# Two chunks share a slot of quarter products: the attention part of a fused retention and gated-FFN kernel, rearranged

## The chip, the cores and the metric

The kernel runs on one core of a Trainium2 chip. The metric is the device time of one execution in microseconds (us). A core has TensorE (PE in the profile; its weight loads are PEld), VectorE (DVE), ScalarE (ACT), GpSimd (POOL) and SyncE (SP), each with an instruction stream of its own that runs in order. Matrix products are accumulated in the eight banks of PSUM; the other operands lie in SBUF.

## What is computed

A retention layer (attention without softmax, with a decay in place of it) over 8 batches, 8 heads, 576 positions and 64 elements per head, and behind it a gated feed-forward network on its 4608 rows of 512 elements:

```python
def _attn_ref(q, k, v):                       # each [8, 8, 576, 64], float32
    scores = (1/sqrt(64)) * q @ k.transpose(0, 1, 3, 2)
    gamma = 1.0 - 2.0 ** (-5.0 - arange(8))   # one decay per head
    rel = pos[:, None] - pos[None, :]
    Dmat = where(rel >= 0, gamma[:, None, None] ** rel, 0.0)
    return (scores * Dmat) @ v

def _moe_ref(x, w_gate, w_val, w_out):        # x [4608, 512]; weights 512x1536, 512x1536, 1536x512
    gate = 1.0 / (1.0 + exp(-(x @ w_gate)))
    val = x @ w_val
    return (gate * val) @ w_out
```

Because the decay is a power of the distance, retention can be worked out in chunks: within a piece of 64 positions by masked scores (intra), and from all earlier positions through a state, the sum of k times v over them (inter). The powers of gamma are multiplied into q and k when they are cast to bf16.

## The kernel before

Everything on the way is bf16 with fp32 sums. `xT` holds the output of retention, transposed, as the input of the network. The network works in blocks of columns of `xT` (256, 384, 384 and then 512 columns): for each block 12 pairs of h products (gate and value, one pair per 128 of the 1536 hidden elements), then output products, 128 rows at a time, in three pieces of four. The retention of later columns is done in between: 30 chunks of 128 positions, each of two pieces (`j` = 0, 1) of 64. The products of a chunk use quarters of the array (64x64), so four of them, one per quarter, lie beside each other. Row half `y` of the array takes its operands from partitions 64y to 64y+63; column half `x` writes partitions 64x to 64x+63.

One **slot** carries, in TensorE's order, the values of the chunk before (intra, then inter), and the scores and state products of the next one:

```python
    ROWS = [(qk_psum, "qk"), (qk_psum, "qk")]      # two banks
    VALS = [(pv_psum, "pv"), (tr_psum, "tr")]      # two banks; ffn_psum has three, st_psum one

    def scores(s):                                  # 16 quarter products
        t = turned[s]
        row_ps[s] = [pool.tile([P, 2, M, 64], FP32, tag=tag, ...) for i, (pool, tag) in enumerate(ROWS)]
        # row_ps[s][y][half(j), 0, m] = k piece j times q piece j, head m of half y

    def products(s):                                # 16: what piece j adds to the state
        # row_ps[s][j][half(y), 1, m] = k piece j times v piece j

    def mask(s):                                    # VectorE, twice: causal mask, to bf16 (probs)
        ...

    def intra(s):                                   # 16
        val_ps[s] = [pool.tile([P, M + 2, 64], FP32, tag=tag, ...) for i, (pool, tag) in enumerate(VALS)]
        # val_ps[s][j][half(x), kc] += v piece j times probs piece j; row half j writes bank j

    def inter(s):                                   # up to 16
        for u in range(2):
            for j in range(NJ):
                if before(s, j) is None:            # the first piece of a batch has no state
                    continue
                for y in range(2):
                    for x in range(2):
                        m = 2 * u + x
                        nc.tensor.matmul(val_ps[s][y][half(x), 2 * y + u if j == y else M + u, :],
                                         lhsT=before(s, j)[half(y), m, :], rhs=turned[s][half(y), 0, m, half(j)],
                                         start=False, stop=(u == 1), skip_group_check=True)

    def slot(s):
        if s > 0:
            intra(s - 1)
            inter(s - 1)
        if s < NS:
            scores(s)
            if STEPS[s][1] < LAST:                  # the last chunk of a batch makes no state
                products(s)
        if s < NS:
            mask(s)
```

Row half `y` writes bank `y` only. Where `j` differs from `y`, the sum belongs to the other bank's values; it goes to two columns of its own (`M + u`), the **share**, and is added when the values are taken out. After a slot, its follow-up work is handed out in three steps, one after each of the next pieces of the network:

```python
    def leave_own(s, j):
        own = slice(2 * j, 2 * j + 2)
        nc.scalar.copy(out=xT[:, own, cols_of(s, j)], in_=val_ps[s][j][:, own])
        if before(s, j) is not None:
            shares[s, j] = nat_pool.tile([P, 2, 64], FP32, tag="share", ...)
            nc.scalar.copy(out=shares[s, j], in_=val_ps[s][1 - j][:, M:M + 2])

    def leave_other(s, j):                          # VectorE: the other two columns plus the share
        ...

    def add_state(s, j):                            # VectorE: running state + row_ps[s][j][:, 1], fp32
        ...

    def after(s, i):                                # i = 0, 1, 2
        makes = s < NS and STEPS[s][1] < LAST
        to_bf16 = on_act if s < 6 else on_pool
        if i > 0 and s > 0:
            leave_other(s - 1, i - 1)
        if i < 2 and s > 0:
            leave_own(s - 1, i)
        if i < 2 and makes:
            add_state(s, i)
        if i > 0 and makes and (s, i - 1) in totals:
            keep_state(..., totals.pop((s, i - 1)), to_bf16)     # the state in bf16
```

The main loop spreads the slots evenly over the pieces of a block:

```python
    BLOCKS = [(512, 256), (768, 384), (1152, 384)] + [(t, 512) for t in range(1536, NT, 512)]
    for w, (t0, n) in enumerate(BLOCKS):
        ...                                         # end: slots by which the next block's columns are ready
        for i, cols in enumerate(ffn_units(t0, n)):
            gone += cols
            ...
            if n > 256 and i % 2 and i < 2 * NFC:
                continue                            # only between a pair of h products and the next
            if pending:
                pending.pop(0)()
            elif slots < end and gone * (end - begin) >= (slots - begin) * (total - 5 * 2048):
                next_slot(slots)                    # slot(s), casts for chunk s + 3, three steps of after
                slots += 1
```

Casting a chunk takes GpSimd three instructions (k, q, v); q and k are then transposed by a DMA into the tile T.

Of the kernel before, what the change touches and what calls it, by code (L numbers as in the profile page):

```python
# [16 lines left out]
def kernel(  # L17
# [268 lines left out]
    def cast_v(s, eng):  # L286
        natural["v", s] = nat_pool.tile([P, H, D], BF16, tag="v", name=f"v_{s}")
        eng(out=natural["v", s], in_=loaded[s][2])  # L288

    def cross(s):  # L290
        t = att_pool.tile([P, 2, M, P], BF16, tag="T", name=f"T_{s}", bufs=5)
        nc.sync.dma_start_transpose(out=t.rearrange("p j m t -> p (j m) t"),
                                    in_=natural_qk[s].rearrange("p j m d -> p (j m d)"))
        turned[s] = t
# [27 lines left out]
    def pair_qk(A, g, banks):  # L322
# [8 lines left out]
        if g == 0:  # L331
            probs["p", A] = att_pool.tile([P, 2, M, 2, P], BF16, tag="ptp", name=f"ptp_{A}", bufs=2)
        for hh in range(2):
            nc.vector.tensor_tensor(out=probs["p", A][:, hh, 2 * g:2 * g + 2], in0=ps[hh],  # L334
                                    in1=trip.unsqueeze(1).to_broadcast([P, 2, 2, P]), op=ALU.mult)
# [33 lines left out]
    def third_intra(banks):  # L369
# [4 lines left out]
        for r in range(2):  # L374
            for u in range(2):
                for y in range(2):
                    for a in range(2):
                        for x in range(2):
                            kc = 2 * y + u
                            nc.tensor.matmul(pair_ps[4 + a][kc][0][half(x), kc, :],  # L380
                                             lhsT=natural["v", 2][half(a), r, head(2, 2 * u + x, y), :],
                                             rhs=probs["p", 2][half(a), y, 2 * u + x, r, :],
                                             start=(a, x) not in begun, stop=(r == 1 and kc == M - 1),
                                             skip_group_check=True)
                            begun.add((a, x))
# [21 lines left out]
    def pair_intra(A, g, a):  # L407
# [3 lines left out]
        for i in range(2):  # L411
            m = 2 * g + i
            ps, at_m, of = pair_ps[s][m]
            for r in range(2):
                for hh in range(2):
                    nc.tensor.matmul(ps[half(hh), at_m, :], lhsT=natural["v", A][half(a), r, 2 * m + hh, :],
                                     rhs=probs["p", A][half(a), hh, m, r, :],
                                     start=(at_m == 0 and r == 0), stop=(at_m == of - 1 and r == 1),
                                     skip_group_check=True)
# [18 lines left out]
    def turn_step(s):  # L438

        t = att_pool.tile([P, 2, M, P], BF16, tag="T", name=f"T_{s}", bufs=5)  # L440
        for i, ((pool, tag), eng) in enumerate(zip(VALS, (on_act, on_dve))):
# [10 lines left out]
    def new_state(key, dt=BF16):  # L452
        final = dt == BF16 and key[1] == LAST - 1 and key[2] == NJ - 1
        tag = "s32" if dt == FP32 else "sf" if final else "sb"
        return nat_pool.tile([P, M, D], dt, tag=tag, name=f"{tag}_{key[0]}_{key[1]}_{key[2]}", bufs=4)

# [18 lines left out]

    def scores(s):
        t = turned[s]
        row_ps[s] = [pool.tile([P, 2, M, 64], FP32, tag=tag, name=f"row_{s}_{i}") for i, (pool, tag) in enumerate(ROWS)]
        for m in range(M):
# [14 lines left out]
    def mask(s):  # L494
        probs[s] = att_pool.tile([P, 2, M, 64], BF16, tag="pt", name=f"pt_{s}")
        for y in range(2):
            nc.vector.tensor_tensor(out=probs[s][:, y], in0=row_ps[s][y][:, 0],  # L497
                                    in1=tri.unsqueeze(1).to_broadcast([P, M, 64]), op=ALU.mult)

    def intra(s):  # L500
        val_ps[s] = [pool.tile([P, M + 2, 64], FP32, tag=tag, name=f"val_{s}_{i}") for i, (pool, tag) in enumerate(VALS)]
        for kc in range(M):
            for j in range(NJ):
                for x in range(2):
                    h = 2 * kc + x
                    nc.tensor.matmul(val_ps[s][j][half(x), kc, :], lhsT=natural["v", s][half(j), h, :],  # L506
                                     rhs=probs[s][half(j), h // M, h % M, :], start=(kc == 0), stop=(kc == M - 1),
                                     skip_group_check=True)

    def inter(s):  # L510


        for u in range(2):
            for j in range(NJ):
                if before(s, j) is None:
                    continue
                for y in range(2):
                    for x in range(2):
                        m = 2 * u + x
                        nc.tensor.matmul(val_ps[s][y][half(x), 2 * y + u if j == y else M + u, :],  # L520
                                         lhsT=before(s, j)[half(y), m, :], rhs=turned[s][half(y), 0, m, half(j)],
                                         start=False, stop=(u == 1), skip_group_check=True)

    def slot(s):

        if s > 0:
            intra(s - 1)
            inter(s - 1)
        if s < NS:
            scores(s)  # L530
            if STEPS[s][1] < LAST:
                products(s)
        if s < NS:
            mask(s)

    def leave_own(s, j):

        own, other = slice(2 * j, 2 * j + 2), slice(2 - 2 * j, 4 - 2 * j)
        nc.scalar.copy(out=xT[:, own, cols_of(s, j)], in_=val_ps[s][j][:, own])  # L539
        if before(s, j) is not None:  # L540
            shares[s, j] = nat_pool.tile([P, 2, 64], FP32, tag="share", name=f"share_{s}_{j}", bufs=4)
# [26 lines left out]
    def after(s, i):  # L568

        makes = s < NS and STEPS[s][1] < LAST  # L570
        to_bf16 = on_act if s < 6 else on_pool
        if i > 0 and s > 0:
            leave_other(s - 1, i - 1)
        if i < 2 and s > 0:
            leave_own(s - 1, i)
        if i < 2 and makes:
            add_state(s, i)
        if i > 0 and makes and (s, i - 1) in totals:
            b, c = STEPS[s]
            keep_state((b, c, i - 1), totals.pop((s, i - 1)), to_bf16)  # L580

# [30 lines left out]
    def next_slot(s):  # L612
# [6 lines left out]
        if s + 1 == 1:  # L619
            pending.insert(2, lambda: turn_step(s + 1))  # L620


# [316 lines left out]

    BLOCKS = [(512, 256), (768, 384), (1152, 384)] + [(t, 512) for t in range(1536, NT, 512)]  # L940
    pieces = 0
    slots = 0
    for w, (t0, n) in enumerate(BLOCKS):
        nxt = BLOCKS[w + 1] if w + 1 < len(BLOCKS) else None
        end = last_step(nxt[0] + nxt[1]) + 2 if nxt else NS + 1
        begin = slots
        total = 2 * NFC * 4 * n + 12 * 512 * (n // P)
        gone = 0
        for i, cols in enumerate(ffn_units(t0, n)):
            gone += cols  # L950
            pieces += 1
            if stores and (nxt is None or w + 2 == len(BLOCKS) and pieces % 4 == 0):
                leave()
            if n > 256 and i % 2 and i < 2 * NFC:
                continue
            if pending:
                pending.pop(0)()
            elif slots < end and gone * (end - begin) >= (slots - begin) * (total - 5 * 2048):
                next_slot(slots)
                slots += 1  # L960
        while pending or slots < end:
            if pending:
                pending.pop(0)()
            else:
                next_slot(slots)
                slots += 1
    while stores:
# [30 lines left out]
```

## Time and profile before

| | |
|---|---|
| time, three runs | 332.96, 334.00, 334.78 us; median 334.0 |
| span of the profiled execution | 330.1 us, TensorE clock 1.00 throughout |
| TensorE busy | 320.9 us |
| h products (two groups) | 100.0 and 100.6 us of busy time |
| output products (512 columns each) | 81.2 us, 379 ns for one |
| quarter products: intra | 480 of 198 ns (overlapping), 9.9 us of busy time |
| mask (VectorE) | 60 of 419 ns |
| gv, the gated product (VectorE) | 96 of 654 ns on average |
| sigmoid (ScalarE) | 96 of 570 ns on average |

A duration in the profile is that of one instruction. Matrix products overlap: the next one starts long before the record of the last ends, so what a product costs TensorE is read from the distance between starts, not from its duration. The timeline merges neighbouring instructions of one kind (x16 are sixteen), and gives the start of the first and the time to the end of the last. In a group, the number after the bar is busy time, the next the mean of one, and then the idle time ahead of it, with what ended it.

### The profile page before, as it was taken

Reading aid. Unit: us, or ns where it says so; the run is one execution under the profiler, and the core shown is the slowest. Engines: PE = TensorE matmul, PEld = TensorE weight load, DVE = VectorE, ACT = ScalarE, POOL = GpSimd, SP = SyncE. Lnnn points to the kernel's source line nnn. Section 1 sums busy time; section 2 is a strip of 40 time slices with the busy share of each in tenths; the row PEclk is TensorE's granted clock in tenths of the full one; section 3 lists DMA queues with packets and bytes.
Section 4 is the critical chain, followed back from the end, with each engine's and each line's share of the span. In section 5 each row is a group of like instructions: output and inputs, shape, how many; then the busy total and the mean of one; then the engine's idle time right before and its main releaser. Section 6 shows DMA issues by size and latency. Waiting matters only on the chain.

```text
span 330.1 us, 8965 instructions
## 1 busy us (share of the span) xinstructions
PE 320.9 (97%) x3663; PEld 172.1 (52%) x3696; DVE 154.9 (47%) x357; ACT 130.2 (39%) x322; POOL 117.2 (35%) x171
## 2 busy tenths in 40 slices
PE   8899999899999999999999999999999999999996
PEld 8764557756646654444444444444444444444443
DVE  6845647666616633552356326541555056304310
ACT  6554545454424433432343333432443233423321
POOL 5684545533545573244224606070434000000000
PEclk9999999999999999999999999999999999999999
DMA  7999999999999999999967897959414900020003
GB/s 215 313 371 370 332 266 218 181 181 160 192 197 164 208 185 267 195 181 260 164 129 101 214 199 92 167 152 191 74 34 110 333 7 2 0 97 33 1 34 95
DMA packets 144794, 55.16 MB, mean 167 GB/s; under 512 B 125168, under 2 KB 136688, under 8 KB 144752
## 3 DMA queue, kind: packets, MB, share of 16 engines
q1 hardware_dynamic: 144608, 54.44, 79.7%
q8 instruction: 29, 0.48, 0.6%
q10 hardware_dynamic: 144, 0.13, 0.1%
q14 instruction: 13, 0.11, 0.1%
HBM read 37.75 MB, written 9.44 MB: 143 GB/s over the span
## 4 chain that ended last, share of the span: by engine, by line
PE 95%; ACT 2%; DVE 1%; issue 1%; ACTq 0%
PE h L638 50%; PE op L705 23%; PE op L892 3%; PE hv L742 3%; PE hg L742 3%; PE val L506 2%; PE idle L182 2%; PE row L490 1%; PE row L482 1%; PE val L520 1%; PE op L694 1%; PE qkp L329 1%; ACT qT L320 1%; PE hg L821 1%; PE st L348 1%
## 5 line engine op out<-in xcount | busy, mean ns | idle before, releaser
L638 PE MATMUL h<-xT,wv_sb 128*128 128x512 bf16 (+2 forms) x416 | 100.0, 355 | 0.8
L638 PE MATMUL h<-xT,wg_sb 128*128 128x512 bf16 (+2 forms) x431 | 100.6, 355 | 0.2
L666 DVE TENSOR_TENSOR gv<-g,h 128x512 bf16<-128x512 bf16 (+1 forms) x96 | 62.8, 654 | 65.1 <-PE h L638 62.4
L662 ACT ACTIVATE g<-h 128x512 bf16<-128x512 f32 (+1 forms) x96 | 54.8, 570 | 97.1 <-PE h L638 96.7
L705 PE MATMUL op<-wo_sb,gv 128*128 128x512 bf16 x361 | 81.2, 379 | 1.3 <-issue 1.1
L638 PEld LDWEIGHTS <-wg_sb 128*128 128x128 bf16 x432 | 41.9, 98 | 41.5 <-DVE xT L550 0.6
L638 PEld LDWEIGHTS <-wv_sb 128*128 128x128 bf16 x432 | 40.6, 98 | 37.3
L705 PEld LDWEIGHTS <-gv 128*128 128x128 bf16 x372 | 35.8, 98 | 42.1
L497 DVE TENSOR_TENSOR pt<-row,tri 128x256 bf16<-128x256 f32 x60 | 22.6, 419 | 63.1 <-PE row L490 55.7
L459 POOL CAST sb<-s 128x256 bf16<-128x256 f32 x35 | 14.0, 400 | 102.4 <-DVE s L563 70.4
L681 ACT COPY ob<-op 128x512 f32<-128x512 f32 x33 | 19.3, 585 | 56.7 <-PE op L705 51.2
L283 POOL TENSOR_TENSOR qk<-k,ktab 128x512 bf16<-128x512 f32 x30 | 31.3, 1042 | 23.1 <-DMA k<-in_k_dram 14.8
L283 POOL TENSOR_TENSOR qk<-q,qtab 128x512 bf16<-128x512 f32 x28 | 29.2, 1042 | 2.4 <-DMA q<-in_q_dram 1.8
L288 POOL CAST v<-v 128x512 bf16<-128x512 f32 x29 | 17.7, 609 | 10.7 <-DMA v<-in_v_dram 8.5
L550 DVE TENSOR_TENSOR xT<-val,share 128x128 bf16<-128x128 f32 x54 | 15.4, 285 | 9.0 <-ACT share L542 9.0
L539 ACT CAST xT<-val 128x128 bf16<-128x128 f32 x60 | 15.7, 263 | 8.7 <-PE val L520 8.7
L542 ACT COPY share<-val 128x128 f32<-128x128 f32 x54 | 15.3, 283 | 2.6 <-DVE xT L550 1.5
L563 DVE TENSOR_TENSOR s<-s,row 128x256 f32<-128x256 f32 x39 | 16.1, 412 | 0.0
L506 PEld LDWEIGHTS <-v 64*64 64x64 bf16 x480 | 6.4, 107 | 12.6 <-issue 12.3
L892 PE MATMUL op<-wo_sb,gv 128*128 128x512 bf16 x45 | 11.4, 379 | 0.3 <-issue 0.2
L506 PE MATMUL val<-pt,v 64*64 64x64 bf16 x480 | 9.9, 198 | 0.8 <-DVE xT L550 0.8
L334 DVE TENSOR_TENSOR ptp<-qkp,trip 128x512 bf16<-128x512 f32 x12 | 7.6, 684 | 4.6 <-PE qkp L329 4.6
(100 smaller groups left out, 240.2 us busy)
## 6 DMA issues: line engine op xcount, KB each, us to landing
out_dram<-ob SPq DMA_DIRECT2D x31, 256.0 KB, 3.1
k<-in_k_dram SPq DMA_DIRECT2D x26, 256.0 KB, 4.8
q<-in_q_dram SPq DMA_DIRECT2D x26, 256.0 KB, 4.6
v<-in_v_dram SPq DMA_DIRECT2D x26, 256.0 KB, 5.2
wg<-in_moe_w_gate_dram SPq DMA_DIRECT2D x12, 256.0 KB, 5.9
wv<-in_moe_w_val_dram SPq DMA_DIRECT2D x12, 256.0 KB, 5.5
wo<-in_moe_w_out_dram SPq DMA_DIRECT2D x12, 256.0 KB, 5.4
k32p<-in_k_dram SPq DMA_DIRECT2D x6, 256.0 KB, 5.5
```

The source lines that it names most:

```text
L283: eng.tensor_tensor(out=natural_qk[s][:, i].rearrange("p m (y d) -> p y m d", y=2), in0=by_halves(loaded[s][1 - i]), in1=tab, op=ALU.mult)
L288: eng(out=natural["v", s], in_=loaded[s][2])
L497: nc.vector.tensor_tensor(out=probs[s][:, y], in0=row_ps[s][y][:, 0], in1=tri.unsqueeze(1).to_broadcast([P, M, 64]), op=ALU.mult)
L506: nc.tensor.matmul(val_ps[s][j][half(x), kc, :], lhsT=natural["v", s][half(j), h, :], rhs=probs[s][half(j), h // M, h % M, :], start=(kc = ...
L563: nc.vector.tensor_tensor(out=new, in0=running[b], in1=p, op=ALU.add)
L638: nc.tensor.matmul(out, lhsT=w_sb[:, kc, fc * P:(fc + 1) * P], rhs=xT[:, kc, t0 + a:t0 + e], start=(kc == 0), stop=(kc == NKC - 1))
L662: nc.scalar.activation(out=g[:, 0:n], in_=h1[:, 0:n], func=AF.Sigmoid)
L666: nc.vector.tensor_tensor(out=gvs[some[0]][:, a:e], in0=g[:, 0:n], in1=h2[:, 0:n], op=ALU.mult)
L681: (eng or on_act)(out=ob, in_=opp)
L705: nc.tensor.matmul(opp, lhsT=gvs[fc][:, nb * P:(nb + 1) * P], rhs=wo_sb[:, fc, :], start=(fc == 0), stop=(fc == NFC - 1))
L742: nc.tensor.matmul(ps, lhsT=(wg_sb if what == "g" else wv_sb)[:, kc, fc * P:(fc + 1) * P], rhs=xT[:, kc, 0:4 * P], start=(kc == 0), stop=( ...
L892: nc.tensor.matmul(opps[nb], lhsT=gvs[fc][:, nb * P:(nb + 1) * P], rhs=wo_sb[:, fc, :], start=(fc == 0), stop=(fc == NFC - 1))
```

## The change

From the block at column 1152 on, a slot takes two chunks (`slot_of_two`), and it is placed among the output products only. The first three blocks keep 4, 3 and 1 single slots.

In a slot of two, the values of both chunks lie in the same two banks, eight columns of 64 in each, and there are no shares: each inter product adds straight to where its sum belongs. For that, both row halves write each bank[...]. So the inter products fall into two families: first those of a row half's own bank, behind the intra products; then VectorE reads one column of each bank (`glance`); then, after the scores and state products of the two new chunks, those of the other bank. The reads tie the two families: the second may only start when VectorE has seen the first. The values leave by one ScalarE copy per chunk and piece. The second new chunk's scores take the bank of `st` and one of the three `ffn` banks.

The single slots keep the shares, but ScalarE copies both in the first step of the follow-up work and its own columns later, so that ScalarE and VectorE read different banks at a time. Buffers grow: v from 5 to 6, T from 5 to 6 (shared with ptp, now two tiles in place of one), pt from 3 to 4, bf16 states from 4 to 8. The core of the diff:

```diff
@@ cast_v, cross, turn_step, new_state, mask: numbers of buffers, as above (cut)
-    def scores(s):
+    def scores(s, banks=None):
         t = turned[s]
-        row_ps[s] = [... for i, (pool, tag) in enumerate(ROWS)]
+        row_ps[s] = [... for i, (pool, tag) in enumerate(banks or ROWS)]
...
-    def inter(s):
+    def inter(s, js, apart=False):
         for u in range(2):
-            for j in range(NJ):
-                if before(s, j) is None:
-                    continue
-                for y in range(2):
+            for y in range(2):
+                for j in js[y]:
+                    if before(s, j) is None:
+                        continue
                     for x in range(2):
                         m = 2 * u + x
-                        nc.tensor.matmul(val_ps[s][y][half(x), 2 * y + u if j == y else M + u, :],
-                                         lhsT=before(s, j)[half(y), m, :], rhs=turned[s][half(y), 0, m, half(j)],
-                                         start=False, stop=(u == 1), skip_group_check=True)
+                        out_ = val_ps[s][y][:, M + u] if apart and j != y else val_ps[s][j][:, 2 * y + u]
+                        nc.tensor.matmul(out_[half(x)], lhsT=before(s, j)[half(y), m, :],
+                                         rhs=turned[s][half(y), 0, m, half(j)], start=False, stop=(u == 1),
+                                         skip_group_check=True)
...
+    ROWS_2 = [(st_psum, "st"), (ffn_psum, "ffn")]
+    glance = consts.tile([P, NJ], FP32)
+
+    def slot_of_two(vals, news):
+        if vals:
+            both = values(len(vals) * M, vals[0])
+            for i, s in enumerate(vals):
+                val_ps[s] = [t[:, i * M:(i + 1) * M] for t in both]
+                intra(s, i == 0)
+                inter(s, [(0,), (1,)])
+            for j in range(NJ):
+                nc.vector.tensor_copy(out=glance[:, j:j + 1], in_=both[j][:, 0, 0:1])
+        for s, banks in zip(news, (ROWS, ROWS_2)):
+            scores(s, banks)
             if STEPS[s][1] < LAST:
                 products(s)
+        for s in vals:
+            inter(s, [(1,), (0,)])
+        for s in news:
             mask(s)
 
+    def after_two(vals, news, i):
+        if i < NJ:
+            for s in vals:
+                nc.scalar.copy(out=xT[:, :, cols_of(s, i)], in_=val_ps[s][i])
+        for n, s in enumerate(news):
+            b, c = STEPS[s]
+            if c == LAST:
+                continue
+            if i == n:
+                add_state(s, 0)
+                add_state(s, 1)
+            if i == n + 1:
+                for j in range(NJ):
+                    if (s, j) in totals:
+                        keep_state((b, c, j), totals.pop((s, j)), on_act)
...
     def after(s, i):                     # single slots
-        if i > 0 and s > 0:
-            leave_other(s - 1, i - 1)
-        if i < 2 and s > 0:
-            leave_own(s - 1, i)
-        if i < 2 and makes:
-            add_state(s, i)
-        ...
+        if i == 0:
+            if s > 0:
+                leave_share(s - 1, 0)
+                leave_share(s - 1, 1)
+            if makes:
+                add_state(s, 0)
+        else:
+            if s > 0:
+                leave_other(s - 1, i - 1)
+                leave_own(s - 1, 2 - i)
+            if i == 1 and makes:
+                add_state(s, 1)
+            ...                          # keep_state as before
...
+    def next_two(vals, news):
+        slot_of_two(vals, news)
+        if news:
+            casts_to(news[-1] + LEAD_CAST + 1)
+        for i in range(3):
+            pending.append(lambda i=i: after_two(vals, news, i))
...
+    SINGLE = [4, 3, 1]
     for w, (t0, n) in enumerate(BLOCKS):
...                                      # twos: the pairs (vals, news) of this block, none for w < 2
             if pending:
                 pending.pop(0)()
             elif slots < end and gone * (end - begin) >= (slots - begin) * (total - 5 * 2048):
                 next_slot(slots)
+                valued = slots - 1
                 slots += 1
+            elif twos and i - n_h >= (0 if len(twos) > 1 else 5 if n < 512 else 6):
+                next_two(*twos[0])
+                valued = twos[0][0][-1]
+                slots = max([slots] + [s + 1 for s in twos.pop(0)[1]])
```

## The prediction

> **What bounds the kernel now.** I read the page from the top, first the busy shares and slices, then the chain that ended last and the groups:
>
> ```profile
> PE 320.9 (97%) x3663; PEld 172.1 (52%) x3696; DVE 154.9 (47%) x357; ACT 130.2 (39%) x322; POOL 117.2 (35%) x171
> ...
> PE   8899999899999999999999999999999999999996
> ...
> PEclk9999999999999999999999999999999999999999
> ...
> PE 95%; ACT 2%; DVE 1%; issue 1%; ACTq 0%
> ...
> L550 DVE TENSOR_TENSOR xT<-val,share 128x128 bf16<-128x128 f32 x54 | 15.4, 285 | 9.0 <-ACT share L542 9.0
> L539 ACT CAST xT<-val 128x128 bf16<-128x128 f32 x60 | 15.7, 263 | 8.7 <-PE val L520 8.7
> L542 ACT COPY share<-val 128x128 f32<-128x128 f32 x54 | 15.3, 283 | 2.6 <-DVE xT L550 1.5
> L563 DVE TENSOR_TENSOR s<-s,row 128x256 f32<-128x256 f32 x39 | 16.1, 412 | 0.0
> ```
>
> TensorE is busy in every slice, at full clock, and 95% of the chain is TensorE: the end is set by how long its in-order stream takes. VectorE and ScalarE are under half busy, so what the change saves there counts only where TensorE waits for it.
>
> Busy TensorE is not TensorE at its best, so I went to the TensorE timeline around two slots in a block of 512 columns:
>
> ```profile
> 125.19 1.03 PE L638 MATMUL h<-xT,wg_sb 128*128 128x512 bf16 x4
> 126.14 0.32 PE L506 MATMUL val<-pt,v 64*64 64x64 bf16 x16
> 126.29 0.30 PE L520 MATMUL val<-T,sb 64*64 64x64 bf16 x16
> 126.42 0.30 PE L482 MATMUL row<-T 64*64 64x64 bf16 x16
> 126.66 1.04 PE L638 MATMUL h<-xT,wv_sb 128*128 128x512 bf16 x3
> ...
> 132.71 1.03 PE L638 MATMUL h<-xT,wg_sb 128*128 128x512 bf16 x4
> 133.66 0.32 PE L506 MATMUL val<-pt,v 64*64 64x64 bf16 x16
> 133.81 0.30 PE L520 MATMUL val<-T,sf 64*64 64x64 bf16 x16
> 133.94 0.30 PE L482 MATMUL row<-T 64*64 64x64 bf16 x16
> 134.07 0.36 PE L490 MATMUL row<-v,qk 64*64 64x64 bf16 x16
> ```
>
> Four products of 512 columns start every 0.216 us: their merged 1.03 us is three steps and one duration of 0.379, and (1.03 - 0.379)/3 is 0.217. The group of 132.71 therefore starts its last at 133.36 and would let a next one start at 133.57. The slot's first quarter product starts at 133.66, **0.09 us late**. The 64 quarter products start over 0.58 us (133.66 to about 134.24, which is 134.07 + 0.36 less one duration of 0.19): 9 ns each. The next full-array product starts at 134.36, **0.12 us after the last quarter product**. A slot of 64 thus costs 0.79 us, of which about 0.20 is entering and leaving, if the last quarter's own 8 ns is left out. The slot at 126.14 lacks the products of L490: next due at 126.06, resumed at 126.66, 0.60 us for 48. Sixteen state products then cost 0.18 and the other kinds 0.13 each, which again leaves 0.20 for the two borders. (After most slots the trace lacks the record of one large product: 416 of 432 for wv, where all 432 weight loads are there. In the timeline that looks like 0.22 us lost; I don't count it.)
>
> Adding, over all pairs of neighbouring large products, what exceeds their normal step gives next to nothing beyond slots and missing records. One slot does wait, slot 2 in the 256-column block. The timeline of all engines there:
>
> ```profile
> 62.47 0.28 DVE L550 TENSOR_TENSOR xT<-val,share 128x128 bf16<-128x128 f32 x1
> ...
> 62.79 0.27 ACT L542 COPY share<-val 128x128 f32<-128x128 f32 x1 [0.53 <-DVE xT L550]
> 62.95 0.41 ACT L459 CAST sb<-s 128x256 bf16<-128x256 f32 x1
> 63.26 0.66 ACT L652 ACTIVATE g<-h 128x256 bf16<-128x256 f32 x2
> ...
> 63.67 0.42 DVE L654 TENSOR_TENSOR gv<-g,h 128x256 bf16<-128x256 bf16 x1 [0.59 <-ACT g L652]
> ...
> 64.01 0.28 DVE L550 TENSOR_TENSOR xT<-val,share 128x128 bf16<-128x128 f32 x1
> ...
> 64.35 0.31 PE L506 MATMUL val<-pt,v 64*64 64x64 bf16 x14 [0.84 <-DVE xT L550]
> ```
>
> ScalarE's copy of the second share waited 0.53 us for a VectorE reader of the same bank; cast, sigmoid, gv and the last xT add moved back with it, and TensorE lost 0.84 us before it could reuse the value bank.
>
> [...] 0.09 and 0.12 us at the borders, and no gap where L506, L520, L482 and L490 follow each other. [...] From the groups above, 412 ns at 256 columns and 285 at 128 leave 158 ns at zero columns; I use that.
>
> **The change, part by part.**
>
> *Fewer slots (on the path).* Before there are 31 slots (30 chunks, and the values trail by one). After: 4 + 3 + 1 single slots in the first three blocks, then two slots of two in each of the blocks from column 1152 to 3584, six blocks, so 12. 20 instead of 31: 11 pairs of borders fewer, 11 x 0.20 = **2.2 us less**. The number of quarter products is the same (16 + 16 + 16 + 16 a chunk, less where there is no state), at the same 9 ns.
>
> *The look (on the path only where it isn't covered).* In a slot of two, TensorE writes the intra products and the inter products of its own row half, then VectorE copies one column of each of the two banks, and TensorE's remaining inter products wait for that. From the last start of the first family: to VectorE's start 0.26 us (the slot at 149 shows 149.85 for the mask after a last product at 149.59); two looks of 0.158 us, the second starting about 0.08 after the first, as neighbouring masks start 0.34 apart at 0.42 each: 0.24; back to TensorE 0.06 (64.29 to 64.35 above). Round trip 0.56 us. Beneath it TensorE issues scores and state products of the two new chunks, 2 x (0.13 + 0.18) = 0.62: covered, with 0.06 to spare. I still charge 0.04 for each of eight such slots, since VectorE may be a little late. In three slots the second chunk is the last of a batch, whose L490 products are left out: 0.44 of cover, 0.12 lost each. The last slot of two has no new chunks: 0.56 lost. Sum 0.32 + 0.36 + 0.56 = **1.2 us more**.
>
> *Single slots reordered.* Both shares are copied ahead of the readers they waited for, and at later steps ScalarE and VectorE read different banks. In the stretch shown, the sigmoid could start some 0.6 us earlier, and so the release of the bank: **0.6 us less** of the 0.84. The other seven single slots show no wait worth more than 0.15, so there is nothing more to gain.
>
> *Off the path.* ScalarE's four reads of 263 and 283 ns per chunk become two of 128x256 (about 0.37 each); two VectorE adds of 285 go; the bf16 state casts move from GpSimd to ScalarE (0.41 each). In the output-product stretch these engines do little: from 148.05 to 159.40 VectorE is busy 2.6 and ScalarE 2.5 of 11.35 us. VectorE's train after a slot of two is 4 masks and 4 state adds at 0.34 apart, done some 4 us after the slot began; the next slot of two comes five or six output pieces of 0.86 later, 5.7 us at the least. Row banks, probabilities and states are then ready. The ffn bank lent to a row tile is free again by the same time, before its turn in the rotation of three.
>
> Sum: 334.0 - 2.2 + 1.2 - 0.6 = **332.4 us**.
>
> **Rivals.** *The look waits behind other work.* The first slot of two in a block comes one output piece (0.86 us) after the last h product; the last gv (0.69 us on VectorE, starting 0.27 after its product) is then just over, so VectorE is free when the look is due. If it were not, every first slot would lose up to 0.7 us: 6 x 0.7 = 4 us, and the time would be about 336. For it: the page puts VectorE waits at the door of ScalarE's sigmoid. Against it: the order just worked out.
>
> *Buffers or transfers tie the pairs together.* Two chunks ahead of use, six T and six v buffers are all full after each slot of two, and casts and transposes come in bursts. If a T came late, TensorE would stop for microseconds, and the time would be 335 to 340. Against it: a T is made at least one slot of two ahead, the first pair apart; GpSimd needs 2 x (1.04 + 1.04 + 0.61) = 5.4 us and a transpose 4.7 us of some 17 us a pair. For it: the DMA slices stand at 9 in the first half of the span.
>
> *Slots cost less among output products than among h products*, or first-half savings on VectorE and ScalarE open more waits than I see: 331. I found no such wait to open.
>
> **Range and chances.** The certain term is 2.2 us, 0.7% of the time; the terms against it are each under 1.5. Runs of the kernel before differ by 1.8 us among themselves, so the range is 330.8 to 334.2. 2% would be 6.7 us, three times all that borders can give: faster by over 2% 0.01, within 2% 0.96, slower by over 2% 0.03, which is the late T.
>
> **What would show it.** Right: 20 slots; among them 12 of two chunks (128 quarter products in a full one), each costing 0.20 for borders; TensorE idle before the second family of inter products near zero where two full chunks are new, about 0.1 in three slots, about 0.55 in the last; the wait of 0.84 at slot 2 down to 0.2 or 0.3. Wrong: idle before the second family of over 0.2 in most slots, a VectorE queue that holds gv or masks in front of the look, TensorE waiting for a T, or quarter products that take more than 9 ns in the new order.

## The result, and the profile after

The changed kernel takes 329.28 us (median; 329.05 to 329.44), the kernel before 333.56 beside it: a ratio of 0.9867, with a 95% interval of 0.9835 to 0.9898. That is 4.3 us less, within the 2% that the prediction called "within", and below its range of 330.8 to 334.2. The predicted gain was 1.6 us, so the prediction missed more than half of it. Measured once more on another occasion, the pair gave 329.17 against 332.41, ratio 0.9894 (0.9864 to 0.9925), 3.2 us; the changed kernel had stayed where it was. So about 1 us of the first 4.3 lay in the four executions of the kernel before, and some 3.2 us are to be explained.

The page of the kernel after, its busy shares, its slices, its chain by engine and the group of the look (count, then busy time, then the mean in ns):

```profile
PE 317.6 (97%) x3662; PEld 172.3 (53%) x3696; DVE 149.1 (46%) x335; ACT 139.3 (43%) x314; POOL 104.1 (32%) x138
...
PE   8899999999999999999999999999999999999995
...
PE 94%; DMA 1%; issue 1%; ACT 1%; DVE 1%; POOL 0%; SPq 0%; ACTq 0%
...
L553 DVE COPY glance<-val 128x1 f32<-128x1 f32 x24 | 2.7, 154 | 23.3 <-PE val L525 22.6
```

TensorE is still what sets the end, its busy time is 3.3 us shorter, and 24 looks of 154 ns have come in: two for each of 12 slots of two.

One such slot in the timeline of all engines (start, time to the end of the last, what):

```profile
145.60 0.32 PE L509 MATMUL val<-pt,v 64*64 64x64 bf16 x16
...
145.94 0.24 PE L525 MATMUL val<-T,sf 64*64 64x64 bf16 x8
...
146.00 0.34 PE L483 MATMUL row<-T 64*64 64x64 bf16 x16
...
146.25 0.22 DVE L553 COPY glance<-val 128x1 f32<-128x1 f32 x2 [0.65 <-PE val L525]
...
146.47 0.35 PE L491 MATMUL row<-v,qk 64*64 64x64 bf16 x16
...
146.64 0.27 PE L525 MATMUL val<-T,sb 64*64 64x64 bf16 x8
...
147.13 0.38 PE L765 MATMUL op<-wo_sb,gv 128*128 128x512 bf16 x1 [0.16 <-issue]
```

The first family ends with starts just before 146.00; VectorE looks from 146.25 to 146.47; the second family starts at 146.64, right behind the last state product (146.47 + 0.35, less one duration of 0.19, is 146.63). The look is covered. After the output product ahead of the slot, the next one was due at 145.51; it starts at 147.13, and 0.22 of that is an output product whose record is missing (355 of 372 are there). That leaves 1.40 us for 128 quarter products, where two single slots of 64 take 1.58: 0.18 less. A second trace of the changed kernel, in which that record is there, gives 1.40 as well.

The last slot of two has nothing new to do, and there the look is bare:

```profile
287.73 0.24 PE L525 MATMUL val<-T,sf 64*64 64x64 bf16 x8
...
288.02 0.23 DVE L553 COPY glance<-val 128x1 f32<-128x1 f32 x2 [3.92 <-PE val L525]
288.30 0.26 PE L525 MATMUL val<-T,sb 64*64 64x64 bf16 x8 [0.33 <-DVE glance L553]
```

The first family's last start is at 287.78 (0.24 less one duration of 0.19, behind 287.73), so the round trip is 0.52 us. The bracket counts only the 0.33 in which no product was in flight.

And slot 2, which had waited 0.84 us for its value bank:

```profile
62.29 0.26 ACT L583 CAST xT<-val 128x128 bf16<-128x128 f32 x1
62.42 0.42 DVE L714 TENSOR_TENSOR gv<-g,h 128x256 bf16<-128x256 bf16 x1
...
62.76 0.28 DVE L597 TENSOR_TENSOR xT<-val,share 128x128 bf16<-128x128 f32 x1
...
63.10 0.31 PE L509 MATMUL val<-pt,v 64*64 64x64 bf16 x14 [0.17 <-DVE xT L597]
```

ScalarE no longer waits here for VectorE's reader (0.53 us before). Counted from the slot's first quarter product (63.30 before, 62.72 here), the last xT add starts after 0.04 us where it had started after 0.71, and TensorE goes on after 0.38 in place of 1.05. In four other traces with the new order and the pairs this slot costs TensorE 1.13 us where it had cost 1.82. In the trace shown it costs 1.46, because 0.34 us pass between two of its state products, at 63.58; nothing in the trace says why.

### The profile page after: what moved, and what is told of

Same layout as the page of the kernel before. It is cut to its first block, busy times and chain, and to the rows that moved or that the text cites. A ratio compares the mean times of both kernels' runs of the same rounds, so it can differ in the third digit from the quotient of the medians.

```text
span 327.4 us, 8876 instructions
## 1 busy us (share of the span) xinstructions
PE 317.6 (97%) x3662; PEld 172.3 (53%) x3696; DVE 149.1 (46%) x335; ACT 139.3 (43%) x314; POOL 104.1 (32%) x138
## 4 chain that ended last, share of the span: by engine, by line
PE 94%; DMA 1%; issue 1%; ACT 1%; DVE 1%; POOL 0%; SPq 0%; ACTq 0%
PE h L698 50%; PE op L765 24%; PE op L952 3%; PE hv L802 3%; PE hg L802 3%; PE val L509 2%; PE row L483 1%; PE row L491 1%; DMA k32p<-in_k_dram 1%; PE val L525 1%; PE op L754 1%; PE hg L881 1%; PE hv L881 1%; PE qkp L329 1%; PE st L348 0%
## 5 line engine op out<-in xcount | busy, mean ns | idle before, releaser
L698 PEld LDWEIGHTS <-wv_sb 128*128 128x128 bf16 x432 | 41.9, 98 | 40.4
L498 DVE TENSOR_TENSOR pt<-row,tri 128x256 bf16<-128x256 f32 x60 | 21.6, 417 | 14.2 <-PE row L491 12.6
L567 ACT CAST xT<-val 128x256 bf16<-128x256 f32 x46 | 15.0, 380 | 22.8 <-PE val L525 21.3
L459 ACT CAST sb<-s 128x256 bf16<-128x256 f32 x44 | 15.9, 420 | 0.5 <-DVE s L610 0.4
L553 DVE COPY glance<-val 128x1 f32<-128x1 f32 x24 | 2.7, 154 | 23.3 <-PE val L525 22.6
L525 PE MATMUL val<-T,sb 64*64 64x64 bf16 x368 | 9.7, 195 | 0.3 <-DVE glance L553 0.3
L809 DVE TENSOR_TENSOR gv<-g,hv 128x512 bf16<-128x512 bf16 x10 | 6.7, 684 | 6.9 <-PE hv L802 6.9
L483 PE MATMUL row<-T 64*64 64x64 bf16 x480 | 9.6, 196 | 0.0
```

Of the source, the lines that this page charges most:

```text
L459: eng(out=state[key], in_=src)
L698: nc.tensor.matmul(out, lhsT=w_sb[:, kc, fc * P:(fc + 1) * P], rhs=xT[:, kc, t0 + a:t0 + e], start=(kc == 0), stop=(kc == NKC - 1))
```

## The experiments

All ratios are to the kernel before, timed on the same chip on the same occasion. There were four such occasions, on three chips, with medians of the kernel before of 332.4 to 332.6 us, so times of different occasions can be compared to some 0.2 us.

**The kernel before once more.**

> The kernel before, unchanged, profiled and timed again. Between the two profiles in hand the span falls by 2.7 us (330.1 to 327.4), between the medians of the times by 4.3. If the other 1.6 us is a wait that the kernel before meets in most of its runs and missed in its first profile, this profile has a span of 331 to 333 us and one TensorE wait of 0.5 to 2 us that the first lacks. If it is only scatter of the chip, the times stay between 331.8 and 334.8 with no wait of that size, and the profile's TensorE timeline differs in the first 10 us alone.

Ratio 1.0007 (0.9990 to 1.0024); the profile has again a span of 330.1 us and the same waits. There is no wait that the first profile missed. The trace differs before its first slot, which starts 0.16 us later, and makes that up in small pieces. The median was 333.05 us here, and 332.4 to 332.6 where the kernel before was timed beside others, so 334.0, from which the prediction counted, was 1.0 to 1.6 too high; the profiled execution, 331.8, had said so.

**The buffers alone.** Only the numbers of buffers change (v and T 6, ptp as two tiles of T, pt 4, bf16 states 8, and the states for the last chunks and in fp32 5, not 4):

```diff
-        natural["v", s] = nat_pool.tile([P, H, D], BF16, tag="v", name=f"v_{s}")
+        natural["v", s] = nat_pool.tile([P, H, D], BF16, tag="v", name=f"v_{s}", bufs=6)
...
```

> The kernel before with the changed numbers of buffers alone (v and T 6, ptp in two tiles, pt 4, bf16 states 8). Theory A (fewer borders between tiling modes, less the look, plus the single slots' order): no change, ratio 1.000 within 0.002. Theory B (the missing 1.6 us was a late T or cast which more buffers remove): 0.994 to 0.996, and a smaller scatter of the times.

0.9994 (0.9967 to 1.0021): nothing. Theory B falls.

**The order alone**, in all 31 single slots:

```diff
-        if i > 0 and s > 0:
-            leave_other(s - 1, i - 1)
-        if i < 2 and s > 0:
-            leave_own(s - 1, i)
+        if i == 0:
+            if s > 0:
+                leave_share(s - 1, 0)
+                leave_share(s - 1, 1)
...
```

> The kernel before with the new order of the follow-up work (both shares copied first) in all of its 31 single slots, nothing else. Theory A: the wait of 0.84 us at slot 2 falls to about 0.45, the small one at slot 3 goes, together 0.8 us: ratio 0.997 to 0.998. Theory C (the order also frees the value banks earlier in later blocks, so that it makes most of the gain): 0.990 to 0.993.

1.0002 (0.9983 to 1.0022), against 0.997 to 0.998 expected. Yet the trace shows the gain: slot 2 costs 1.15 us, not 1.82. It is lost again within 10 us: slot 3 costs 1.10 us, not 0.87, and at the border to the block at column 768 the first h product follows the last output product 0.71 us late (0.27 in the kernel before). The timeline there:

```profile
70.70 1.04 POOL L283 TENSOR_TENSOR qk<-k,ktab 128x512 bf16<-128x512 f32 x1 [2.92 <-DMA k<-in_k_dram]
70.77 2.06 DVE L597 COPY sf<-sbd 64x128 bf16<-64x128 bf16 x2
...
71.73 1.04 POOL L283 TENSOR_TENSOR qk<-q,qtab 128x512 bf16<-128x512 f32 x1
```

Two small VectorE copies (of the first batch's state) take 2.06 us together, about as long as the two GpSimd casts beside them (1.04 each), and the xT adds that the next block needs stand behind them. In the profile of the changed kernel one of them ran beside a cast of v (0.62 us) and the other behind it (0.19), and the first h product was on time. So a copy took 1.03 us here, in the kernel before 0.52 and 1.06 with the same casts beside it, and in the changed kernel 0.19 with no GpSimd instruction beside it. Why it takes longer beside a cast, no trace shows.

**The pairs with the old order in the eight single slots.**

```diff
         if i > 0 and s > 0:
             leave_other(s - 1, i - 1)
         if i < 2 and s > 0:
             leave_own(s - 1, i)
+            leave_share(s - 1, i)
```

> The changed kernel with the follow-up work of its eight single slots in the old order. Theory A: 0.8 us above the changed kernel, so 330 us, ratio to the kernel before 0.989 to 0.991. Theory C: the changed kernel's time plus 2 us or more, ratio 0.993 or above.

0.9922 (0.9897 to 0.9947), 330.03 us: the 330 of theory A, with a ratio just above its 0.991, and below the 0.993 of theory C. The order is worth 0.75 to 0.85 us beside the pairs, and the rest of the change carries the larger part. But why the order counts here and not alone was open.

**The changed kernel once more.**

> The changed kernel itself, timed again beside the kernel before on one chip. The profiles taken so far differ before the first slot as well: it starts between 52.97 us (the changed kernel) and 54.58 us, in code that the change hardly touches. If the 4.3 us between the first medians was partly the luck of few executions, the ratio here is 0.990 to 0.992, so 2.7 to 3.3 us. If the whole of it belongs to the change, 0.986 to 0.988.

0.9894 (0.9864 to 0.9925). The smaller gain, 3.2 us, is the better figure: part of the 4.3 was the few executions.

**Borders doubled.** Slots 11 to 29 of the kernel before, cut in two:

```diff
+        if 11 <= s < NS:
+            pending.append(lambda: rows_part(s))
```

> The kernel before, with each of the slots 11 to 29 cut in two: the values, and one output or h piece later the scores, state products and masks. The work is the same, and there are 19 more pairs of borders between full-array and quarter products. Theory A (a pair of borders costs 0.20 us of TensorE): 3.8 us more, ratio 1.011 to 1.012. Rival (borders are cheap, and the gain of pairs came from elsewhere): under 1 us, ratio below 1.003.

1.0094 (1.0064 to 1.0125): 3.1 us more for 19 pairs of borders. In the TensorE timeline a cut slot reads:

```profile
161.45 0.32 PE L506 MATMUL val<-pt,v 64*64 64x64 bf16 x16
161.59 0.30 PE L520 MATMUL val<-T,sb 64*64 64x64 bf16 x16
161.82 1.04 PE L645 MATMUL h<-xT,wv_sb 128*128 128x512 bf16 x4
```

Each half costs 0.47 us beyond the normal step, the whole had cost 0.79, so a cut costs 0.15; from the last product before slot 4 to the end the trace grew by 3.17 us (259.69 against 256.52), 0.167 for each cut. Borders are real, and cutting a slot costs a fifth less than the 0.20 of the prediction. The lateness at the two ends is all there: each half starts 0.09 us late, and the large product comes 0.12 after its last start. What became cheaper is the state products, whose 16 starts spread over 0.105 us in a half and over 0.176 in most whole slots. Why they are quicker there was not tried.

**The pairs among the h products.**

```diff
@@ after_two
-            if i == n:
+            if i == 0:
                 add_state(s, 0)
                 add_state(s, 1)
...
-            elif twos and i - n_h >= (0 if len(twos) > 1 else 5 if n < 512 else 6):
+            elif twos and i >= ((8 if w == 2 else 4) if len(twos) > 1 else 18 if w == 2 else 14):
```

> The changed kernel with its slots of two among the h products (after the third and eighth pair of a block) in place of the output products; both chunks' state adds are given out in the first step. Theory A says that the place matters through VectorE and the lent ffn bank: masks and state adds queue with the gv products, the row bank in ffn comes free some 4.4 us after the slot's start where an h product needs it after 3.1, so TensorE waits about 1.3 us in each slot: 10 to 15 us more than the changed kernel. Rival (the place is indifferent, the pairing alone counts): the changed kernel's time within 1 us.

0.9964 (0.9950 to 0.9978), 331.45 us: 2.3 us above the changed kernel, far from the 10 to 15 expected. The waits are of the kind foretold (h products that start 0.15 us late behind a slot, 1.07 in the block of 384 columns), but most h products in the blocks of 512 columns start on time. The look waits are the same 0.67 us as among output products. The place is worth 2.3 us, about twice what the pairs gain, and a fifth of what I had expected.

**The last look covered.** Its second family one output piece later:

```diff
-        for s in vals:
-            inter(s, [(1,), (0,)])
+        if news:
+            second_family(vals)
...
+        else:
+            pending.append(lambda: second_family(vals))
```

> The changed kernel, but in the last slot of two, which has no new chunks, the second family of inter products comes one output piece later, so that the look is covered by 0.86 us of products, at the price of one more pair of borders. Theory A: 0.52 us of waiting goes, 0.20 comes, so 0.3 us less in the trace from the seventh slot on (229.6 to 229.3); too little to be sure of in the times. Rival (the wait at the look is shown in the trace but hides in something else): no less, or 0.2 us more.

0.9894 (0.9865 to 0.9922), 329.12 us: no difference to the changed kernel that can be measured. In the trace the last slot fell from 1.26 to 0.95 us, the expected 0.3, while three other slots of two grew by up to 0.14. That is no more than such slots differ between two traces of the changed kernel itself (1.40 and 1.62 us for one of them). Whether it stays better is open.

At this point the sum did not close: pairs 1.2, order 0.8, and over 1 us beyond. What set the kernels apart was the transfers. The packets of 512 B in the traces' first 17 us (loads of q, k and v for the first columns) took a mean of 31 to 32 ns in every kernel without the look, and 27 to 28 in every kernel with it, long before the first look. The look's tile stands among the constants, ahead of all other buffers, and moves them by 32 bytes. No trace shows an address; the places given here are those of the built programs, where all buffers behind the constants (loads, v, qk, T, gv, stores) lie equally far beyond a multiple of 256 bytes and move together. Which of them counts was not tried apart.

**The kernel before with a tile of that size that nobody uses.**

```diff
     xT = consts.tile([P, M, NT], BF16)
+    pad = consts.tile([P, 2], FP32, name="pad")
```

> The kernel before with one unused tile of two fp32 columns among the constants, nothing else. The tile of the look in the changed kernel has this size and stands in this place, and moves every buffer behind it by 32 bytes: loads, T, qk, v and stores then begin at a multiple of 256 bytes in each partition, where before they began 224 beyond one. In the traces so far packets of 512 B take 31 to 32 ns in all kernels without that tile and 27 to 28 ns in all with it. Theory D (the placement is a part of the gain of its own): 27 to 28 ns here, the first slot 0.3 to 0.6 us earlier, the wait at the border to the block at 768 gone, together 0.8 to 1.5 us: ratio 0.9955 to 0.9975. Theory A alone (borders, look and order are all there is): packets may be shorter, but the time stays, ratio 1.000 within 0.0015.

0.9963 (0.9950 to 0.9976), 331.40 us: **1.2 us for an unused tile**. The queue of the transfers and the loads of k (KB each, median us from issue to landing), in the page of the kernel before:

```profile
q1 hardware_dynamic: 144608, 54.44, 79.7%
...
k<-in_k_dram SPq DMA_DIRECT2D x26, 256.0 KB, 4.8
```

and in that of the kernel with the tile:

```profile
q1 hardware_dynamic: 144608, 54.44, 67.4%
...
k<-in_k_dram SPq DMA_DIRECT2D x26, 256.0 KB, 3.7
```

The same packets and bytes take 12 points less of the engines' time. The first slot starts at 53.2 us, not 53.7, and the first h product at the border is on time, where it was 0.27 late: together 0.8 us, which is what the span lost between these two profiles (330.1 to 329.3). The other 0.4 of the 1.2 these two traces don't show. The group of the two VectorE copies, before and with the tile, reads:

```profile
L588 DVE COPY sf<-sbd 64x128 bf16<-64x128 bf16 x2 | 1.6, 786 | 0.0
...
L589 DVE COPY sf<-sbd 64x128 bf16<-64x128 bf16 x2 | 0.4, 184 | 0.0
```

The loads of k land sooner (3.7 us after their issue, not 4.8), and a copy takes 0.18 us, as the one behind its cast did in the changed kernel (0.19). All traces agree on the border: in the eight kernels with the buffers moved its first h product is on time, and in the seven traces of the others that have the full clock throughout it is 0.23 to 0.71 us late. The first slot starts at 53.0 to 54.0 us in the former and at 53.7 to 55.1 in the latter.

**The changed kernel with its buffers where they were.**

```diff
-    glance = consts.tile([P, NJ], FP32)
+    glance = consts.tile([P, 64], FP32)
```

> The changed kernel with the look's tile 64 fp32 columns wide, of which it uses two as before, so that all buffers behind it begin 224 bytes beyond a multiple of 256, as in the kernel before. Theory D: packets of 512 B back at 31 to 32 ns, 0.8 to 1.5 us slower than the changed kernel: 330.0 to 330.7 us, ratio 0.993 to 0.9955. Theory A alone: the changed kernel's 329.2, ratio 0.989 to 0.991.

0.9959 (0.9946 to 0.9973), 330.98 us: 1.8 us given back, packets at 32 ns. That is more than the 0.8 to 1.5 expected and the 1.2 of the unused tile; why it is more stays open. From the last product before the first slot to the end this trace takes 274.35 us, the changed kernel's 274.45, so in these traces placement counts ahead of the first slot alone. (The profiled execution took 333.07 us, with the stretch of half clock described at the end.)

**The tile and the order, without pairs.** The kernel before with both edits:

```diff
+    pad = consts.tile([P, 2], FP32, name="pad")
...
+                leave_share(s - 1, 0)
+                leave_share(s - 1, 1)
...
```

> The kernel before with the unused tile and with the new order of the follow-up work in all single slots: everything of the change but the pairs and the buffer numbers. Theory A with D: the order's gain of 0.7 us at slot 2, which without the tile was lost again at the next block's border, now stays, on top of the tile's: 1.5 to 2.2 us, ratio 0.9935 to 0.9955, and the pairs keep 1.0 to 1.3 us for themselves. Rival (the order gives nothing even so): the ratio of the tile alone.

0.9939 (0.9920 to 0.9959), 330.47 us: 0.9 us below the tile alone. The intervals of the two ratios overlap, but the times themselves don't (330.27 to 330.82 in six executions, 331.01 to 331.45 in nine). The order's gain stays once the border does not take it back; slot 2 costs 1.15 us in this trace, and the border adds nothing.

**A wide look.**

```diff
-                nc.vector.tensor_copy(out=glance[:, j:j + 1], in_=both[j][:, 0, 0:1])
+                nc.vector.tensor_copy(out=glance[:, j], in_=both[j][:, 0:2])
```

> The changed kernel with a look of 128 columns of each bank in place of one (and the small unused tile, to keep the buffers where the changed kernel has them). A look then takes 0.285 us in place of 0.154, the round trip about 0.80 in place of 0.52. Theory A (the scores and state products cover 0.62 us at most): TensorE waits 0.15 us in eight slots of two, 0.35 in three and 0.8 in the last, 2.3 to 2.8 us more than the changed kernel, less the 0.67 it waits already: 1.8 us, so 331 us, ratio 0.995 to 0.997. Rival (TensorE isn't held up by the look, since something else covers it): within 0.4 us of the changed kernel.

0.9957 (0.9943 to 0.9971), 331.16 us, the 331 that theory A expected. The timeline of a slot with two full new chunks:

```profile
180.72 0.49 DVE L554 COPY glance<-val 128x128 f32<-128x128 f32 x2 [0.65 <-PE val L526]
...
181.26 0.32 PE L526 MATMUL val<-T,sb 64*64 64x64 bf16 x16
```

The state products end their starts at 181.09 there, so TensorE waits 0.16 us. Over all 12 slots it waits 2.86 us, where the changed kernel waits 0.67. So a longer look is paid for nearly in full, and nothing else covers it. In the changed kernel little is to spare: in a full slot the second family starts 0.16 us after the look ends, and 0.05 after it in the bare slot, which leaves 0.11.

**Which boundary.** Three paddings of the kernel before, 16, 24 and 40 columns wide:

```diff
+    pad = consts.tile([P, 16], FP32, name="pad")     # 24 and 40 in the other two
```

> The kernel before with an unused tile of 64 bytes in each partition, so that all buffers behind it begin 32 bytes beyond a multiple of 256. Theory D1 (what counts is whether a 256-byte piece starts at a multiple of 256): packets of 512 B at 31 to 32 ns, ratio 1.000 within 0.002. Theory D2 (a multiple of 32 that isn't one of 64 is the trouble): the same, 31 to 32 ns.

> As above with 96 bytes: all buffers behind it begin 64 bytes beyond a multiple of 256. Theory D1: packets of 512 B at 31 to 32 ns, ratio 1.000 within 0.002. Theory D2 (a multiple of 64 is enough): 27 to 28 ns, ratio 0.995 to 0.9975.

> As above with 160 bytes: all buffers behind it begin 128 bytes beyond a multiple of 256. Theory D1: packets of 512 B at 31 to 32 ns, ratio 1.000 within 0.002. Theory D2: 27 to 28 ns, ratio 0.995 to 0.9975.

Ratios 0.9988 (0.9966 to 1.0009), 0.9995 (0.9972 to 1.0019) and 0.9990 (0.9972 to 1.0009); packets of 512 B at 31, 30 to 31 and 29 to 31 ns. Of the five places tried (0, 32, 64, 128 and 224 beyond a multiple of 256) only the multiple itself saves time, so D1 holds for the time and D2 falls. The packets are a little shorter than D1's 31 to 32 ns, and at 128 they come near the 28.4 of the unused tile in the first 17 us (28.9; 30.7 after that, against 27.1). The runs show the effect (32 to 28 ns); why the place of a buffer changes the time of its packets, no run shows.

## Why the prediction was wrong, point by point

| step | predicted | measured | by |
|---|---|---|---|
| base | 334.0 us | 332.4 to 332.6 | later medians of the kernel before |
| 11 pairs of borders fewer | -2.2 | -1.8 | 11 x 0.167, borders doubled |
| the look | +1.2 | +0.67 | waits in the trace |
| order of single slots | -0.6 | -0.9 | tile and order against tile alone |
| place of all buffers | not in the sum | -1.2 | unused tile |
| sum | -1.6 | -3.2 | ratio 0.9894 of 332.4 is 3.5; medians differ by 3.2 |

- **The step that failed is the sum itself, "334.0 - 2.2 + 1.2 - 0.6"**: it takes the 32 bytes of the look's tile for nothing. They moved every load buffer to a multiple of 256 bytes and gave 1.2 us by themselves, of the 1.6 that the sum was short (3.2 measured, 1.6 forecast). Nothing in the page of before says so in words, but two lines held the clue: transfers at 9 for half the span, and, among the groups, a VectorE copy of 64x128 with a mean of 786 ns (720 in the second profile) where a state add of 128x256 takes 412. I had read neither as part of the path, because TensorE was busy throughout. And "next to nothing beyond slots and missing records" passed over the border at column 768, where the trace of before has an h product 0.27 us late.
- **The borders** are as described; the size was a little off. The lateness at both ends (0.09 and 0.12) is there in every half of a cut slot. But the prediction let the quarter products start every 9 ns however they are grouped, and they don't: a cut costs 0.15 to 0.17 in all, and putting two full slots together saves 0.18.
- **The look** had the right round trip (0.56 foretold, 0.52 measured) and the right three cases. With two full new chunks it costs nothing measurable (0.04 charged), where the second has no state products it costs 0.03 to 0.06 (0.12 charged), bare it costs 0.51 (0.56). The term fell to about half, mostly in the padding I had put on. That the two families need an order at all was my assumption: every kernel with the look keeps it, so no run shows what happens without one.
- **The order** gave what slot 2 had lost and a little more. That it depends on the border after it, and the border on where the load buffers lie, I did not see.
- Pairs as such: from the last product before slot 7 on, the traces take 230.89 us with tile and order, and 229.60 and 229.86 in two traces of the changed kernel: 1.0 to 1.3 us less. The measured sizes make it -1.8 + 0.67 = -1.1, and the prediction had -2.2 + 1.2 = -1.0. The mechanism was right; that the sum was right too is partly luck, since both terms were too large.
- The first comparison's other 1 us is scatter of the kernel before; I took the median of three runs as the base though the profiled execution stood 2.2 us below it. Two of the four first times, 334.00 and 334.78, lie where later executions with a lower granted clock lie (333.4 to 335.6, last section); their own clock was not recorded.
- The terms are not strictly additive: the place of the buffers counts 1.2 us without the pairs and 1.8 with them.
- Rivals: the look never waits behind gv (VectorE had been idle for 0.49 us or more ahead of all twelve), and no T came late. The page does not put VectorE's waits at the sigmoid's door, as I had read it: of 65.1 us before gv, 62.4 end with an h product of TensorE. The place among output products matters less than I had expected before its run: 2.3 us.

## What to carry to other kernels

When a change adds or resizes a tile, look at where all the others come to lie, and test the placement by itself with an unused tile before crediting the mechanism: here it was over a third of the gain. Products of 64x64 interleaved with those of the full array cost 0.15 to 0.18 us here per entry and exit, so gather them; an order enforced by another engine's look was free here where 0.64 us of independent products stood over a round trip of 0.52. And a gain at one wait can be eaten at the next one down the stream, so an edit that measures nothing alone is not yet refuted.

## What I had not expected of the hardware

Load buffers 224, 32, 64 or 128 bytes beyond a multiple of 256 gave packets of 512 B with a mean of 29 to 32 ns, buffers on the multiple 27 to 28; those of 256 B behind 90 us took 23 to 25 ns off it and 20 to 22 on it.

A second thing goes with the place of the buffers: in 52 of 313 executions of kernels with buffers off the multiple, and in none of 69 with them on it, TensorE's mean granted clock lies at 0.988 to 0.995, where the others have 0.998 or more. Two traces show it: the clock falls to a half for 6.8 us, which takes 0.010 off the mean. The trace of the changed kernel with its buffers off the multiple has such a stretch (window, then busy time of each engine, then the granted clock, the share and rate of the transfers):

```profile
16.50:23.30 6.80, 6.80 (x90) 5.00 (x88) 1.89 (x4) 3.27 (x9) 5.62 (x12) 0.50 1.06 369
```

The last column but two, 0.50, is the clock. What brings it on was not tried. The stretch ahead of it, 10.0 to 16.5 us, has TensorE busy for 4.91 of 6.5 us in this trace and 4.73 in the other (the tile of 96 bytes), and for 5.38 to 5.68 in the fifteen traces without the fall. That the two went together in two traces is all that is shown.
